# One VectorE operation and two ScalarE passes per weight block, and a written-out order of operations, in a fused attention and gated-MLP kernel

## The chip, the core and the metric

The kernel runs on one core of one Trainium2 chip. The metric is the device time of one execution in microseconds (us); the time given for a kernel is the median of its runs. The engines are TensorE (PE, with its weight loads listed as PEld), VectorE (DVE), ScalarE (ACT), GpSimd (POOL) and SyncE (SP), which issues the transfers. Each engine works through its own instruction list strictly in order, so an instruction that waits holds up everything behind it on that engine.

## The reference

Three stages follow each other. All inputs and the output are 32-bit in the reference; the input arrays arrive as 64-bit floats.

```
k_sum, v_sum = k.blocks(32).max(), v.blocks(32).mean()          # 2 x 8 heads, 768 positions, width 64
scores = [scale * q k^T where |i-j| < 16 else -1e9 , scale * q k_sum^T + log 32]
attn = softmax(scores) @ [v ; v_sum]                             # -> x: 1536 tokens x 512
xn = x / sqrt(mean(x*x) + 1e-6) * rms_g
h  = silu(xn @ w_gate) * (xn @ w_val) ; x = h @ w_out            # 512 -> 1536 -> 512
g  = elu(x @ w_in2) ; out = g @ w_out2                           # 512 -> 2048 -> 512
```

## The kernel before

Tokens are worked in three blocks of 512. Attention goes in pairs of 64-query tiles ("pair" j of batch b): copied keys `ka`, scores `s`, row maxima `nm`, exponentials `e` on ScalarE, a division, a transpose `at` on PE, its copy `ats`, and the product `pv` that is copied into `xT`. The first four pairs make block 0. While blocks 1 and 2 go through attention, block 0 goes through the first MLP (12 chunks: `pg`, `pv_..c` products, gate `th`, down product into `acc`) and the second MLP (16 chunks: `ph`, `ex`, down product into `acc`). Afterwards blocks 1 and 2 go through both MLPs together by a Strassen-Winograd scheme: seven products per unit are added up in the PSUM banks A, B and C (`A_1u` is bank A of the first MLP's up stage, `d` the down stage). Between two products into one bank VectorE or ScalarE reads the bank: B is seeded with A after product 0, `h2` and `h4` are saved from B, and `c11`, then `c10`, are combined from C and `h4`, C and `h2`.

The weights arrive as 64-bit floats, in 68 blocks `st` of 128 x 512. Each is made 32-bit once, for block 0, into `raw`: `convert_a` (ScalarE, line 448) moves the exponent, `convert_b` (VectorE, line 456) shifts the high word by three bits, `convert_d` (VectorE, line 469) adds the rest of the low word. The result is then split into a rounded part (ScalarE, line 317) and a remainder (line 328, on VectorE or POOL), both for PE, and `keep` stores it for the joint stage.

The order on each engine comes from a list scheduler inside the kernel (`Order.issue`): it plays the operations with costs and due times, and a table `SHIFT` moves the due times of operation kinds in time ranges. `keep_warm` puts matmuls on zeros where PE would be idle early.

Of the kernel before, what the change touches and what calls it, by code (L numbers as in the profile page):

```python
# [28 lines left out]
SHARED = (  # L29
    "add_square", "diagonal", "x_lo", "x_hi", "act_a", "act_b", "elu_c", "x_sum", "w_sum", "factor_a", "factor_b",  # L30
    "wide_b", "half_sum", "pair_sum", "pair_b", "gate_b2", "gate_c2", "convert_a", "convert_b", "convert_c",
    "convert_d", "split_a", "split_b", "copy_keys", "normalize")

LIGHT = {"mean_v": 0.7, "mean_own": 0.7, "apply_v2": 0.65}

TILED = {"mean_v": 1, "mean_own": 1, "apply_v2": 2, "scores": 3}  # L40
DRAIN_IN, DRAIN_OUT = 0.12, 0.12


class Order:

    DMA_START, DMA_DONE = 1.3, 1.7
    DONE = {"fetch": 1.9, "keep": 0.7, "keep_sum": 0.7, "load_half": 1.0, "again": 0.9, "store": 0.7, "load_v": 1.2}  # L50
    ISSUE = {"load_vtok": 0.5, "load_v": 0.5}
    TICK, WARM = 3.4133, 1.275

    def __init__(self, look, urgent, busy):
        self.look, self.urgent, self.busy = look, urgent, busy
# [12 lines left out]
    def pe_end(self, now, cost, weight, ticks):

        while cost > 1e-9:  # L70
            k = int(now / self.TICK + 1e-9)
            rate = 1.0 if ticks.get(k - 1, 0) >= self.WARM else 0.5
            part = min(cost, ((k + 1) * self.TICK - now) * rate)
            ticks[k] = ticks.get(k, 0) + part * weight
            cost -= part
            now += part / rate
# [4 lines left out]

    def issue(self):
        ops = self.ops
        n = len(ops)
        before = [set() for _ in range(n)]
        writer, readers, home, maker, users = {}, {}, {}, {}, {}
        queue = {}
        for i, (engine, _, due, _, _, r, w, new) in enumerate(ops):
            for tag, name in new:
                home[name] = tag  # L90
                if tag in self.slots and self.slots[tag][1]:
                    queue.setdefault(tag, []).append((due, i, name))
            for key in r:
                before[i].add(writer[key])
                readers.setdefault(key, []).append(i)
            for key in w:
                if key in writer:
                    before[i].add(writer[key])
                before[i].update(readers.pop(key, ()))
                writer[key] = i  # L100
            before[i].discard(i)
            for name in {key.split("#")[0] for key in (*r, *w)} | {name for _, name in new}:
                if name in home:
                    before[i].add(maker.setdefault(name, i))
                    users.setdefault(name, set()).add(i)
            before[i].discard(i)
        queue = {tag: [name for _, _, name in sorted(x)] for tag, x in queue.items()}
        after = [[] for _ in range(n)]
        left = [len(b) for b in before]
        for i, b in enumerate(before):  # L110
            for j in b:
                after[j].append(i)

        ready_at = [op[2] if op[0] in ("SP", "-") else 0.0 for op in ops]
        free = {tag: bufs for tag, (bufs, _) in self.slots.items()}
        busy, soon, started, port = dict(self.busy), {}, [], 0.0
        dma_free = now = 0.0
        events = [(t, -1, 0) for t in (*ready_at, *busy.values()) if t > 0]
        heapq.heapify(events)
        taken = [None] * n  # L120
        ticks = {}
        tiled = 0

        def offer(i):
            for engine in ops[i][0] if isinstance(ops[i][0], dict) else (ops[i][0],):
                soon.setdefault(engine, []).append(i)

        for i in range(n):
            if not left[i]:
                offer(i)  # L130


        def pick(i):
            need, found = {}, []
            for tags, name in ops[i][7]:
                for tag in tags if isinstance(tags, tuple) else (tags,):
                    n = need.get(tag, 0) + 1
                    if free[tag] >= n and (not self.slots[tag][1] or name in queue[tag][:n]):
                        break
                else:  # L140
                    return None
                need[tag] = n
                found.append((tag, name))
            return found

        def can(i):
            return pick(i) is not None

        def shared(i, engine):
            return engine in ("DVE", "POOL") and ops[i][3].__name__ in SHARED  # L150

        while len(started) < n or events:
            for engine in list(soon):
                if busy.get(engine, 0.0) > now + 1e-9:
                    continue
                todo = sorted((i for i in soon[engine] if taken[i] is None), key=lambda i: (ops[i][2], i))
                best = next((
                    i for i in todo if ready_at[i] <= now + 1e-9 and can(i)
                    and (not shared(i, engine) or port <= now + 1e-9)), None)
                if best is None:  # L160
                    continue
                where, cost, due, _, _, _, _, new = ops[best]
                if isinstance(where, dict):
                    cost = where[engine]
                look = now + self.look * cost
                if engine != "SP" and any(
                        ops[i][2] < due - self.urgent and now < ready_at[i] <= look and can(i) for i in todo):
                    continue
                taken[best] = engine
                for e in where if isinstance(where, dict) else (where,):  # L170
                    soon[e].remove(best)
                for tag, name in pick(best):
                    home[name] = self.tag_of[name] = tag
                    free[tag] -= 1
                    if self.slots[tag][1]:
                        queue[tag].remove(name)
                if engine == "SP":
                    dma_free = max(now + self.DMA_START, dma_free) + cost
                    busy[engine] = now + self.ISSUE.get(ops[best][3].__name__, 0.42)
                    end = dma_free + self.DONE.get(ops[best][3].__name__, self.DMA_DONE)  # L180
                else:
                    if engine == "PE":
                        name = ops[best][3].__name__
                        start = now
                        if TILED.get(name, 0) != tiled:
                            tiled = TILED.get(name, 0)
                            start += DRAIN_IN if tiled else DRAIN_OUT
                        end = self.pe_end(start, cost, LIGHT.get(name, 1.0), ticks)
                    else:
                        end = now + cost  # L190
                    busy[engine] = end
                if shared(best, engine):
                    port = end
                heapq.heappush(events, (end + (0.2 if engine == "PE" else 0.13), best, 1))
                heapq.heappush(events, (busy[engine], -1, 0))
                started.append(best)
                for j in after[best]:
                    left[j] -= 1
                    ready_at[j] = max(ready_at[j], end + self.hop(engine, ops[j][0]))
                    if not left[j]:  # L200
                        offer(j)
                        heapq.heappush(events, (ready_at[j], -1, 0))
# [4 lines left out]
            if ends:  # L207
                for name in {key.split("#")[0] for key in (*ops[i][5], *ops[i][6])} | {x for _, x in ops[i][7]}:
                    if name in users:
                        users[name].discard(i)  # L210
                        if not users[name]:
                            del users[name]
                            free[home[name]] += 1
# [1436 lines left out]
```

## Time and profile before

| | |
|---|---|
| median of 3 runs | 590.2 us (590.08 to 590.88) |
| profiled execution, span of instructions | 589.1 us |
| PE busy | 575.6 us, 98% |
| VectorE busy | 545.4 us, 93% |
| ScalarE busy | 408.6 us, 69% |
| GpSimd busy | 96.2 us, 16% |

An engine is counted busy while an instruction is in it, matmuls with a modelled end, so that a busy PE may still hide short gaps. The span leaves out about 1.1 us that lies around it in the median time.

### The profile page before, as it was taken

What the parts mean: (1) busy time and instruction counts of PE and PEld (TensorE: products, weight loads), DVE (VectorE), ACT (ScalarE), POOL (GpSimd) and SP (SyncE); (2) the same over time, 40 slices, a digit from 0 to 9 for tenths busy, and PEclk for the clock granted to TensorE, in tenths of its full rate; (3) what the DMA queues carried; (4) which work ended last, traced back from release to release, by engine and by line L of the source; (5) the groups of instructions that cost most, each with busy time, mean ns of one, the idle gap of its engine ahead of it and who ended that gap; (6) DMA issues with size and microseconds to landing.
All of it is one profiled execution on the core that took longest, in us unless ns stands there. A gap on an engine that the chain in (4) does not pass through costs nothing.

```text
span 589.1 us, 10067 instructions
## 1 busy us (share of the span) xinstructions
PE 575.6 (98%) x3382; PEld 470.5 (80%) x3382; DVE 545.4 (93%) x1048; ACT 408.6 (69%) x888; POOL 96.2 (16%) x144
## 2 busy tenths in 40 slices
PE   6899999999999999999999999999999999999997
PEld 3688877888788888888888888788888888888886
DVE  4989998889999998999989888999999999999994
ACT  4978749765989889375455446596667599977651
POOL 5755376453311103000000000000000000000000
PEclk9999999999999999999999999999999999999999
DMA  8688899769779799323433453231205525816021
GB/s 312 232 270 305 290 368 327 238 207 298 249 252 303 238 369 333 122 95 121 171 105 118 144 167 120 90 107 55 72 18 203 191 73 170 264 51 214 1 72 53
DMA packets 56052, 108.80 MB, mean 185 GB/s; under 512 B 6784, under 2 KB 19584, under 8 KB 56000
## 3 DMA queue, kind: packets, MB, share of 16 engines
q1 hardware_dynamic: 56000, 108.16, 55.0%
q8 instruction: 26, 0.43, 0.3%
q14 instruction: 26, 0.21, 0.1%
HBM read 79.82 MB, written 28.31 MB: 184 GB/s over the span
## 4 chain that ended last, share of the span: by engine, by line
PE 86%; DVE 6%; DMA 3%; ACT 3%; issue 1%; SPq 0%; POOL 0%; DVEq 0%; POOLq 0%; ACTq 0%
PE acc L966 13%; PE ph L910 8%; PE B_1u L1137 7%; PE B_2u L1137 6%; PE B_2d L1316 6%; PE A_1u L1137 5%; PE C_1u L1137 5%; PE B_1d L1316 4%; PE pg L910 4%; PE A_2u L1137 4%; PE C_2d L1316 4%; PE C_2u L1137 4%; PE A_2d L1316 4%; PE C_1d L1316 3%; PE pv L721 2%; PE A_1d L1316 2%
## 5 line engine op out<-in xcount | busy, mean ns | idle before, releaser
L1137 PE MATMUL B_1u<-xh,w_1u 128*128 128x512 f32 x144 | 48.9, 389 | 0.0
L910 PE MATMUL ph<-xa,ws_i 128*128 128x512 f32 x192 | 45.9, 392 | 0.0
L910 PEld LDWEIGHTS ph<-xa,ws_i 128*128 128x128 f32 x192 | 35.7, 188 | 7.7 <-issue 0.2
L910 PE MATMUL pg<-xs,ws_g 128*128 128x512 f32 (+1 forms) x168 | 37.0, 366 | 0.2 <-DVE th L934 0.2
L1137 PE MATMUL C_1u<-xh,w_1u 128*128 128x512 f32 x96 | 33.4, 390 | 1.1 <-DVE c_1u L1129 1.1
L317 ACT CAST wd<-rd 128x512 fp32r<-128x512 f32 x49 | 29.6, 619 | 5.5 <-PE A_1d L1316 2.8
L1137 PE MATMUL A_1u<-xh,w_1u 128*128 128x512 f32 x96 | 33.1, 389 | 0.0
L328 DVE TENSOR_TENSOR wd<-rd,wd 128x512 fp32r<-128x512 f32 x49 | 33.1, 685 | 0.0
L1137 PE MATMUL B_2u<-xh,w_2u 128*128 128x512 f32 x96 | 32.8, 391 | 0.0
L1316 PE MATMUL B_2d<-td,wd 128*128 128x512 f32 x144 | 32.8, 389 | 0.0
L910 PEld LDWEIGHTS pg<-xs,ws_g 128*128 128x128 f32 x168 | 27.9, 189 | 5.9 <-issue 0.8
L1137 PEld LDWEIGHTS B_1u<-xh,w_1u 128*128 128x128 f32 x144 | 27.0, 188 | 5.6
L1316 PEld LDWEIGHTS B_2d<-td,wd 128*128 128x128 f32 x144 | 27.0, 188 | 5.6
L317 ACT CAST td<-z 128x512 fp32r<-128x512 f32 x28 | 16.7, 620 | 16.9 <-DVE z L1298 16.7
L1137 PE MATMUL B_1u<-xl,w_1u 128*128 128x512 f32 x72 | 28.0, 389 | 0.0
L699 POOL TENSOR_TENSOR e<-e,rs 128x480 f32<-128x480 f32 x20 | 21.1, 1063 | 39.2 <-DVE rs L694 23.8
L684 ACT ACTIVATE e<-e,nm 128x120 f32<-128x120 f32 x64 | 24.4, 384 | 1.0 <-DVE nm L677 0.9
L1316 PE MATMUL B_1d<-td,wd 128*128 128x512 f32 x108 | 24.6, 389 | 0.0
L1316 PEld LDWEIGHTS B_1d<-td,wd 128*128 128x128 f32 x108 | 20.3, 188 | 4.2
L317 ACT COPY h_1u<-B_1u 128x512 f32<-128x512 f32 x22 | 12.9, 588 | 14.8 <-PE B_1u L1137 13.5
L1316 PE MATMUL A_2d<-td,wd 128*128 128x512 f32 x96 | 22.2, 389 | 0.0
L1137 PEld LDWEIGHTS C_1u<-xh,w_1u 128*128 128x128 f32 x96 | 18.0, 188 | 5.3 <-DVE c_1u L1129 1.6
(530 smaller groups left out, 1771.9 us busy)
## 6 DMA issues: line engine op xcount, KB each, us to landing
st_i<-in_moe_w_in SPq DMA_DIRECT2D x16, 512.0 KB, 5.3
st_p<-in_moe_w_out SPq DMA_DIRECT2D x16, 512.0 KB, 5.5
st_v<-in_moe_w_val SPq DMA_DIRECT2D x12, 512.0 KB, 4.8
st_g<-in_moe_w_gate SPq DMA_DIRECT2D x12, 512.0 KB, 6.6
st_o<-in_moe_w_out SPq DMA_DIRECT2D x12, 512.0 KB, 5.0
kept_p<-raw_p SPq DMA_DIRECT2D x16, 256.0 KB, 5.3
kept_i<-raw_i SPq DMA_DIRECT2D x16, 256.0 KB, 5.8
va<-in_v SPq DMA_DIRECT2D x20, 192.0 KB, 6.0
```

Of the source, the lines that this page charges most:

```text
L317: nc.scalar.copy(out=out, in_=in_)
L328: (nc.gpsimd if eng == POOL else nc.vector).tensor_sub(out, a, b)
L684: nc.scalar.activation(out=e[:, pr, :], in_=s[:, pr, :], func=AF.Exp, bias=nm[:, pr:pr + 1], accum_out=ss[:, pr:pr + 1])
L699: nc.gpsimd.tensor_mul(e, e, rs.unsqueeze(2).to_broadcast([P, NP, NK]))
L721: nc.tensor.matmul(pv[64 * h:64 * h + 64, pr, n, :], va[:NK, 2 * pr + h, :], T[f"ats{b}_{j}_{h}"][:, pr, QT * n:QT * n + QT], start=True, ...
L910: nc.tensor.matmul(pt[:, i], wt[:, a, kk * P:(kk + 1) * P], xt[:, c, i], start=(kk == 0 and n == 0), stop=(kk == KM - 1 and n == 2))
L966: nc.tensor.matmul(acc, wt[:, a, cs], ot[e], start=(first and n == 0), stop=(last and n == 2))
L1137: nc.tensor.matmul(pt, wt[:, a, cs], xt[e][:, kk], start=first and kk == n == 0, stop=kk == 1 and n == 2, skip_group_check=not first)
L1316: nc.tensor.matmul(pt[:, h], wt[:, a, cs], xt[:, e, h], start=first and n == 0, stop=last and n == 2 and h.stop == TB, skip_group_check=i ...
```

## The change

`convert_b` and `convert_d` become one VectorE operation, and a second ScalarE pass, `convert_l`, prepares the low word for it: it reads the upper 16 bits of the low word, scales them and writes a whole number of 0 to 7 into the low word's place. The VectorE operation then shifts the high word by three and ORs the two. The scheduler, its costs and `SHIFT` go; `PLAN` lists the operations in order of issue with the chosen engine, `TAGS` the chosen buffers. Costs and due times still stand in the calls but are no longer read. Small edits follow: a new dependency names the selector constants, and the loads of the first queries and weights lose their special cases.

```
-        ops = self.ops
-        n = len(ops)
...
-        for i in started:
-            if i not in later:
-                emit(i)
-        return now
+        picks = iter(TAGS)
+        for code in PLAN:
+            i, choice = divmod(code, 4)
+            engine, _, _, fn, args, _, _, new = self.ops[i]
             for tag, name in new:
...
+                self.tag_of[name] = tag[int(next(picks))] if isinstance(tag, tuple) else tag
+            fn(*((list(engine)[choice],) if isinstance(engine, dict) else ()), *args)
...
+    def convert_l(eng, kind, c):
+        nc.scalar.activation(
+            out=words(kind, c, 0), in_=words(kind, c, 1, U16), func=AF.Copy, scale=0.875 * 2.0 ** -13, bias=0.49)
 
     def convert_b(kind, c):
-        hi = words(kind, c)
-        t = new("raw", f"raw_{kind}{c}", [P, 512], U32)
-        if kind in SIGNED:
-            nc.vector.tensor_scalar(t, hi, 3, None, op0=ALU.logical_shift_left)
...
-    def convert_d(kind, c):
-        rest = T[f"st_{kind}{c}"].bitcast(U16).rearrange("p (n w) -> p n w", w=4)[:, :, 1]
-        low = T[f"raw_{kind}{c}"].bitcast(U16).rearrange("p (n w) -> p n w", w=2)[:, :, 0]
-        nc.vector.scalar_tensor_tensor(low, rest, 2.0 ** -13, low, op0=ALU.mult, op1=ALU.add)
+            new("raw", f"raw_{kind}{c}", [P, 512], U32), words(kind, c), 3, words(kind, c, 0),
+            op0=ALU.logical_shift_left, op1=ALU.bitwise_or)
...
-        add({ACT: 0.57}, 0, need - 8, convert_a, kind, c, r=[st], w=[st])
-        add(DVE, 0.34, need - 7, convert_b, kind, c, r=[st], w=[raw], new=[("raw", raw)])
...
-        add(DVE, 0.63, need - 6, convert_d, kind, c, r=[st, raw], w=[raw])
+        add({ACT: 0.57}, 0, need - 8, convert_a, kind, c, r=[st], w=[st + "#a"])
+        add({ACT: 0.57}, 0, need - 7.5, convert_l, kind, c, r=[st], w=[st + "#l"])
+        add(DVE, 0.63, need - 7, convert_b, kind, c, r=[st + "#a", st + "#l"], w=[raw], new=[("raw", raw)])
...
-SHIFT = {
...
+PLAN = (
+    0, 108, 836, 112, 28, 12, 56, 68, 32, 264, 40, 8, 4, 44, 88, 184, 1648, 64, 60, 76, 72, 48, 52, 196, 189, 194, 80,
...
```

The counts over the whole program, as the built kernels list them: PE has the same 2962 instructions in both. VectorE loses the 68 shifts; 13 of the 29 full-size remainders on POOL move to VectorE (POOL 29 to 16, VectorE's full-size tensor-tensor operations 447 to 460), and so do 3 divisions of exponentials (POOL 20 to 17) and some key copies. ScalarE goes from 791 to 852.

Three places of the order follow. The first is ScalarE in the first attention pairs, from the first key copies to the exponentials of pair 1 (`e_1_0`), before:

```order
L323 ACTIVATE ka_1_266<-ksum_177 128x4x24
L448 ACTIVATE st_v_200<-st_v_200 128x512
L448 ACTIVATE st_g_217<-st_g_217 128x512
L323 ACTIVATE ka_4_309<-kT_0_178 128x4x16
L323 ACTIVATE ka_4_309<-kT_1_190 128x4x80
L323 ACTIVATE ka_4_309<-ksum_177 128x4x24
L684 ACTIVATE e_0_0_278,ss_0_0_321<-s_0_0_262,nm_0_0_301 128x120 x4
L684 ACTIVATE e_0_1_279,ss_0_1_329<-s_0_1_270,nm_0_1_316 128x120 x4
L448 ACTIVATE st_o_221<-st_o_221 128x512
L323 ACTIVATE ka_6_372<-kT_1_190 128x4x96
L323 ACTIVATE ka_6_372<-ksum_177 128x4x24
L684 ACTIVATE e_1_0_341,ss_1_0_389<-s_1_0_296,nm_1_0_365 128x120 x4
```

and in the changed kernel (lines 259 and 262 are `convert_a` and `convert_l`, 467 the exponentials):

```order
L141 ACTIVATE ka_1_238<-ksum_197 128x4x24
L259 ACTIVATE st_v_222<-st_v_222 128x512
L262 ACTIVATE st_v_222<-st_v_222 128x512
L467 ACTIVATE e_0_0_248,ss_0_0_308<-s_0_0_230,nm_0_0_275 128x120 x4
L467 ACTIVATE e_0_1_249,ss_0_1_322<-s_0_1_244,nm_0_1_291 128x120 x4
L262 ACTIVATE st_v_300<-st_v_300 128x512
L259 ACTIVATE st_v_300<-st_v_300 128x512
L467 ACTIVATE e_1_0_337,ss_1_0_360<-s_1_0_268,nm_1_0_358 128x120 x4
```

The key copies `ka_4` and `ka_6` have left ScalarE, and one weight block less is begun, each with two passes.

The second place is ScalarE in the first MLP, around the gates of its chunks 4 and 6 (`th_4`, `th_6`), before:

```order
L448 ACTIVATE st_v_1270<-st_v_1270 128x512
L930 ACTIVATE th_4_1402<-th_4_1402 128x512
L317 CAST ws_g_1423<-raw_g_1399 128x512
L448 ACTIVATE st_o_1360<-st_o_1360 128x512
L317 CAST ws_v_1468<-raw_v_1421 128x512
L317 CAST ws_o_1471<-raw_o_1207 128x512
L317 CAST ws_g_1482<-raw_g_1236 128x512
L317 CAST ws_v_1488<-raw_v_1304 128x512
L448 ACTIVATE st_g_1409<-st_g_1409 128x512
L684 ACTIVATE e_0_0_1429,ss_0_0_1516<-e_0_0_1429,nm_0_0_1480 128x120 x4
L930 ACTIVATE th_6_1514<-th_6_1514 128x512
```

and in the changed kernel, from the gate of chunk 4 to the next attention exponentials (line 713 is the gate):

```order
L262 ACTIVATE st_v_1278<-st_v_1278 128x512
L259 ACTIVATE st_g_1251<-st_g_1251 128x512
L713 ACTIVATE th_4_1291<-th_4_1291 128x512
L259 ACTIVATE st_v_1278<-st_v_1278 128x512
L262 ACTIVATE st_v_1253<-st_v_1253 128x512
L259 ACTIVATE st_v_1253<-st_v_1253 128x512
L467 ACTIVATE e_1_0_1257,ss_1_0_1344<-e_1_0_1257,nm_1_0_1323 128x120 x4
L135 COPY xT_1079<-pv_5_1353 128x4x128
L135 CAST ws_g_1403<-raw_g_1351 128x512
L135 CAST ws_v_1406<-raw_v_1349 128x512
L259 ACTIVATE st_o_1298<-st_o_1298 128x512
L713 ACTIVATE th_5_1398<-th_5_1398 128x512
```

Between gates there are now more conversion passes, and they stand ahead of the casts of later blocks.

The third place is PE at the end of the joint first MLP's up stage, where the last unit's products 5 and 6 go into its bank C (`xh_5`, `xh_6` are the token parts of the products), before:

```order
L1137 MATMUL C_1u_4726<-xh_5_3482,w_1u_4504 128x512
L1137 MATMUL C_1u_4726<-xl_5_3530,w_1u_4504 128x512
L1137 MATMUL C_1u_4726<-xh_5_3482,w_1u_4504 128x512 x2
L1137 MATMUL C_1u_4726<-xl_5_3530,w_1u_4504 128x512
L1137 MATMUL C_1u_4726<-xh_5_3482,w_1u_4504 128x512
L1137 MATMUL C_1u_4726<-xh_6_3560,w_1u_4536 128x512
L1137 MATMUL C_1u_4726<-xl_6_3704,w_1u_4536 128x512
L1137 MATMUL C_1u_4726<-xh_6_3560,w_1u_4536 128x512 x2
L1137 MATMUL C_1u_4726<-xl_6_3704,w_1u_4536 128x512
L1137 MATMUL C_1u_4726<-xh_6_3560,w_1u_4536 128x512
```

and in the changed kernel, from the last matmuls of the last unit's product 5 on:

```order
L920 MATMUL C_1u_4695<-xl_5_3619,w_1u_4467 128x512
L920 MATMUL C_1u_4695<-xh_5_3397,w_1u_4467 128x512
L920 MATMUL C_1u_4622<-xh_6_3615,w_1u_4543 128x512
L920 MATMUL C_1u_4622<-xl_6_3709,w_1u_4543 128x512
L920 MATMUL C_1u_4622<-xh_6_3615,w_1u_4543 128x512 x2
L920 MATMUL C_1u_4622<-xl_6_3709,w_1u_4543 128x512
L920 MATMUL C_1u_4622<-xh_6_3615,w_1u_4543 128x512
L1099 MATMUL A_1d_4661<-td_0_2_4463,wd_01_4682 128x512 x3
L1099 MATMUL A_1d_4719<-td_0_0_4506,wd_00_4631 128x512 x3
L1099 MATMUL A_1d_4719<-td_0_1_4516,wd_00_4631 128x512 x3
```

Product 6 of another unit and ten groups of the down stage's first product now stand between products 5 and 6 of the same bank.

## Rows read from the trace of the kernel before

**Rows 1.** Stretches of the run: busy us and instructions of each engine, PE clock, DMA.
```profile
0.00:44.00 44.00, 35.95 (x498) 26.82 (x499) 33.54 (x83) 30.88 (x113) 25.46 (x67) 0.96 0.81 271
44.00:229.00 185.00, 184.26 (x1315) 150.81 (x1314) 170.55 (x327) 146.18 (x346) 68.16 (x76) 1.00 0.85 290
229.00:260.00 31.00, 31.00 (x142) 25.55 (x141) 29.95 (x62) 17.67 (x33) 2.54 (x2) 1.00 0.38 131
...
400.00:550.00 150.00, 150.00 (x662) 123.64 (x661) 149.94 (x282) 116.06 (x220) 0.00 (x0) 1.00 0.40 129
550.00:589.00 39.00, 35.53 (x163) 29.46 (x161) 30.68 (x52) 14.38 (x24) 0.00 (x0) 0.99 0.13 48
sum 589.00, PE 575.60 PEld 470.46 DVE 545.39 ACT 408.59 POOL 96.17; mean PE 95.93 PEld 78.41 DVE 90.90 ACT 68.10 POOL 16.03
```
**Rows 2.** PE's longest wait that is no first load: us in total, times, longest.
```profile
PE at L709 <- ACT e L684: 2.0, 1, 2.0
```
**Rows 3.** PE at the end of the up stage, and VectorE there, in time.
```profile
378.68 0.39 PE L1137 MATMUL C_1u<-xl,w_1u 128*128 128x512 f32 x1
378.91 0.39 PE L1137 MATMUL C_1u<-xh,w_1u 128*128 128x512 f32 x1
380.44 0.50 PE L1137 MATMUL C_1u<-xh,w_1u 128*128 128x512 f32 x1 [1.14 <-DVE c_1u L1129]
...
379.70 0.68 DVE L1129 TENSOR_TENSOR c_1u<-C_1u,h_1u 128x512 f32<-128x512 f32 x1
```
**Rows 4.** VectorE and then ScalarE in time: conversions and casts that follow each other.
```profile
32.50 0.42 DVE L456 TENSOR_SCALAR raw_v<-st_v 128x512 uint32<-128x512 uint32 x1
32.84 0.42 DVE L456 TENSOR_SCALAR raw_g<-st_g 128x512 uint32<-128x512 uint32 x1
...
33.77 0.74 DVE L469 SCALAR_TENSOR_TENSOR raw_v<-st_v,raw_v 128x512 uint16<-128x512 uint16 x1
34.39 0.73 DVE L469 SCALAR_TENSOR_TENSOR raw_g<-st_g,raw_g 128x512 uint16<-128x512 uint16 x1
...
45.73 0.61 ACT L317 CAST ws_o<-raw_o 128x512 fp32r<-128x512 f32 x1
46.25 0.69 ACT L448 ACTIVATE st_o<-st_o 128x512 f32<-128x512 f32 x1
46.83 0.67 ACT L448 ACTIVATE st_g<-st_g 128x512 f32<-128x512 f32 x1
```
**Rows 5.** GpSimd's remainders: duration in ns (min/median/max), first and last start.
```profile
L328 POOL TENSOR_TENSOR ws_g<-raw_g,ws_g x12: 1278/1298/1698, 39.4 to 139.5; 128x512 fp32r<-128x512 f32 x12
```
**Rows 6.** ScalarE's `convert_a` alone (line 448): busy us and count, PE clock, DMA.
```profile
44.00:229.00 185.00, 39.51 (x60) 1.00 0.85 290
229.00:260.00 31.00, 1.35 (x2) 1.00 0.38 131
```
**Rows 7.** ScalarE before its first exponentials, and PE in the opening, in time.
```profile
11.79 0.60 ACT L323 ACTIVATE ka<-kT 128x64 f32<-128x64 f32 x2
...
12.47 0.34 ACT L684 ACTIVATE e<-s,nm 128x120 f32<-128x120 f32 x1
...
9.66 1.05 PE L668 MATMUL s<-ka,q 64*64 64x120 f32 x32
...
27.66 1.25 PE L709 MATMUL at<-ident,e 128*120 128x128 f32 x8 [1.96 <-ACT e L684]
```
**Rows 8.** Two stretches of the opening, columns as in the first group.
```profile
28.00:30.00 2.00, 2.00 (x29) 1.67 (x29) 1.70 (x7) 1.57 (x7) 0.51 (x2) 0.60 0.00 0
30.00:32.00 2.00, 2.00 (x26) 1.55 (x24) 0.80 (x2) 0.97 (x2) 1.54 (x2) 0.55 0.32 103
```
**Rows 9.** What ScalarE waited for between 44 and 229 us: total, times, longest.
```profile
ACT ws_v L317 <- DVE raw_v L469: 7.0, 5, 3.0
ACT xT L317 <- PE pv L721: 4.8, 2, 4.5
ACT th L930 <- DVE th L927: 4.6, 4, 2.2
```

More of the change, by code (lines that the diff above doesn't have):

```diff
@@ L25, with __init__ @@
 NEG = -1000000000.0
[L29 to L41, printed above, removed]
-class Order:
[L49 to L55, printed above, removed]
+class Order:
+    def __init__(self):
         self.ops = []
@@ L63, in add @@
     def add(self, engine, cost, due, fn, *args, r=(), w=(), new=()):
-        due += SHIFT.get((fn.__name__, sum(due >= x for x in EDGES)), 0)
         self.ops.append((engine, cost, due, fn, args, tuple(r), tuple(w), tuple(new)))
[L68 to L76, printed above, removed]
-        return now
@@ L79, in hop @@
-    def hop(self, a, b):
-        return (0.0 if a == b else 0.2) if a == "PE" else 0.13
-    def issue(self):
-        ops = self.ops
-        n = len(ops)
[L85 to L88, printed above, removed]
-            for tag, name in new:
[L90 to L202, printed above, removed]
-            if not events:
-                stuck = [(e, [(ops[i][2], ops[i][3].__name__, ops[i][4][:3]) for i in t[:3]]) for e, t in soon.items()]
-                raise RuntimeError(f"no group can start: {stuck} {free}")
-            now, i, ends = heapq.heappop(events)
[L207 to L213, printed above, removed]
-        def find(name, *some):
-            return next(i for i in started if ops[i][3].__name__ == name and set(some) <= set(map(str, ops[i][4])))
-        held = {}
-        for late, first in HOLD:
-            held.setdefault(find(*first), []).append(find(*late))
-        later = {j for x in held.values() for j in x}
-        def emit(i):
-            ops[i][3](*((taken[i],) if isinstance(ops[i][0], dict) else ()), *ops[i][4])
-            for j in held.get(i, ()):
-                emit(j)
-        for i in started:
-            if i not in later:
-                emit(i)
-        return now
@@ L254, in fused_kernel @@
     log_b = math.log(BLOCK)
-    o = Order(LOOK, URGENT, {"POOL": 2.1, "DVE": 3.1, "ACT": 2.0, "SP": 0.8})
+    o = Order()
     add = o.add
@@ L381, in fused_kernel @@
     for var in (1, 0, 2):
-        add(POOL, 1.5, 5.0 + var, make_mask, var, r=[] if var == 1 else ["mask1"], w=[f"mask{var}"])
+        add(POOL, {1: 1.5, 0: 0.46, 2: 2.86}[var], 5.0 + var, make_mask, var, r=[] if var == 1 else ["mask1"], w=[f"mask{var}"] + ["sel"] * (var == 2))
     for var in range(2):
@@ L473, in add_weights @@
         add("SP", 1.6, need - (14 if need > T0 + 20 else LEAD), fetch, kind, c, w=[st], new=[("st", st)])
-        add({ACT: 0.57}, 0, need - 8, convert_a, kind, c, r=[st], w=[st])
-        add(DVE, 0.34, need - 7, convert_b, kind, c, r=[st], w=[raw], new=[("raw", raw)])
-        if kind not in SIGNED:
-            add(DVE, 0.6, need - 6.5, convert_c, kind, c, r=[st, raw], w=[raw])
-        add(DVE, 0.63, need - 6, convert_d, kind, c, r=[st, raw], w=[raw])
+        add({ACT: 0.57}, 0, need - 8, convert_a, kind, c, r=[st], w=[st + "#a"])
+        add({ACT: 0.57}, 0, need - 7.5, convert_l, kind, c, r=[st], w=[st + "#l"])
+        add(DVE, 0.63, need - 7, convert_b, kind, c, r=[st + "#a", st + "#l"], w=[raw], new=[("raw", raw)])
         add("SP", 0.67, need + KEEP, keep, kind, c, r=[raw], w=[f"kept_{kind}{c}"])
@@ L539, in add_k @@
             kt = f"kT{b}_{j}"
-            add("SP", 1.4, due - 4 + 1.5 * j, load_first, b, j, w=[kt], new=[("x", kt)])
+            add("SP", 1.4, due - 4 + 1.5 * j, load_k, b, j, w=[kt], new=[("x", kt)])
             for r in range(2):
@@ L747, in add_pair @@
             near = [f"kT{b}_{x}" for x in range(lo // (2 * P), (hi - 1) // (2 * P) + 1)]
-            add({POOL: 0.78, DVE: 0.45, ACT: 0.65} if early else [{POOL: 0.78}, {POOL: 0.78, ACT: 0.65}][KEYS if i >= FLEX else 0], 0, due, copy_keys, b, t,
+            add({POOL: 0.86, DVE: 0.45, ACT: 0.65} if early else [{POOL: 0.86}, {POOL: 0.86, ACT: 0.65}][KEYS if i >= FLEX else 0], 0, due, copy_keys, b, t,
                 r=near + far, w=[f"ka{b}_{t}"], new=[("ka", f"ka{b}_{t}")])
@@ L767, in add_pair @@
                 w=[f"e{n}", f"ss{n}"], new=[("ss", f"ss{n}")])
-            add(DVE, 0.08, at + 4, guard, b, f"{j}_{h}", w=[f"ss{n}"])
+            add(DVE, 0.13, at + 4, guard, b, f"{j}_{h}", w=[f"ss{n}"])
             add(DVE, 0.1, at + 4, invert, b, f"{j}_{h}", r=[f"ss{n}"], w=[f"rs{n}"], new=[("rs", f"rs{n}")])
@@ L1095, in half_sum @@
     def half_sum(sa, sb, blocks, dst):
-        a11, a12, a21, a22 = (part(x) for x in blocks)
+        a11, a12, a21, a22 = blocks
         name, i = (sa, int(dst[1]) - 1) if dst in ("s1", "s2") else (sb, int(dst[1]) - 3)
@@ L1429, in fused_kernel @@
     add("-", 0.0, 0, take, "act", "rk0", [P, TB], w=["rk0"], new=[("act", "rk0")])
-    for i, at in enumerate(WARM_AT):
-        add("-", 0.0, at, wait, w=[f"w{i}"])
-        add(PE, 0.44, at, keep_warm, i, r=[f"w{i}"], new=[(BANKS, f"warm{i}")])
     for i in range(VA):
@@ L1435, in fused_kernel @@
     add_k(0, K0, 0.7)
+    for i, at in enumerate(WARM_AT):
+        add(PE, 0.44, at, keep_warm, i, r=[f"kT0_{AFTER_K[i]}"] if i in AFTER_K else [], new=[(BANKS, f"warm{i}")])
     add_vsum(0, VS0, VS0 + MEAN, BANKS)
```

176 lines of the change are left out of this document (15 added, 161 removed), and 150 rows, old and new, of the table PLAN.

## The prediction

> **What bounds the kernel.** I read the stretches of the run first, then PE's waits, then single places in time. In the stretches the reader is to see that PE is the bound: it is busy 575.6 of 589 us, and what is left lies at the two ends: 8.05 us of PE idle before 44, 0.74 between 44 and 229, none from 400 to 550 although VectorE is busy 149.94 of 150 us there, and 3.47 in the last 39 [rows 1]. PE's list holds the same 2962 matmuls in both kernels, so the time can fall only by PE's idle, by gaps too short to show as idle, and by time at a low clock. A matmul of 128 x 512 shows 0.39 us and the next one starts 0.23 us after it, so a gap of up to 0.16 us is hidden in "busy" [rows 3]. PE's longest wait that is no first load is 2.0 us on exponentials in the opening [rows 2]. The longest in the joint stages is 1.14 us of idle for VectorE's combine of bank C, from start to start 380.44 - 378.91 - 0.23 = 1.30 us [rows 3].
>
> **The conversion.** Two VectorE shifts that follow each other start 0.34 us apart, two `convert_d` 0.62 us apart [rows 4]. The new VectorE operation is not in this trace. It is a pass over 512 elements like both: the bounds are 0.34 (as cheap as the shift) and 0.74 (a whole `convert_d`, nothing overlapped). I take 0.62, since it reads two sources, as `convert_d` does. So the shift alone is saved: 68 x 0.34 = 23.1 us of VectorE; the bounds make it 15 to 42. The Trainium skill, "VectorE: DVE Perf Modes", section "The perf-mode tier table", says that a 32-bit operation on one source runs at twice the rate of one on two, so the change would remove the cheap member of the pair. The rows agree, 0.34 beside 0.62; by that rule the saving would be an estimated 68 x 0.31 = 21 us in place of 23.
>
> The second ScalarE pass is not in this trace either. The nearest row is `convert_a`, a pass over the same strided block: 0.58 us from start to start. Bounds: 0.52, a cast's spacing, and 0.69, a `convert_a` with nothing overlapped [rows 4]. I take 0.58, as reading and writing every other word is what the two share: 68 x 0.58 = 39.4 us more ScalarE (35 to 47).
>
> **The order.** The 13 remainders that move from POOL (1.30 us each, [rows 5]) take about 0.68 us on VectorE, as its combine does [rows 3], or 0.62 in a row, so 8.1 us; for the 3 divisions and some small key copies I put 4 us, by an estimate from their sizes at the same time per element. VectorE's net is -23.1 + 8.1 + 4 = -11 us. None of this is PE time by itself: VectorE full to the brim from 400 to 550 cost PE nothing [rows 1]. The further ScalarE time is hidden too, as long as ScalarE has idle to put it in.
>
> That cover, stage by stage. Between 44 and 229 ScalarE is busy 146.2 of 185 us [rows 1], and 60 of the 68 `convert_a` run there [rows 6]. As many second passes are 60 x 0.58 = 34.8 us, which gives 181.0 of 185, or 98%, if everything stayed in its place. With the next 31 us, where it is busy 17.7 us and two more run, it is 199.8 of 216, or 92%. So the room is there only if the order spreads work towards 260 and keeps ScalarE's waits small. The order does put passes between gates and ahead of later casts, as the second place of the order shows; what queues behind a waiting ScalarE instruction there are gates, exponentials and casts that PE needs soon. I charge PE +0.4 us for the middle (bounds -1, if POOL's slower remainders no longer delay a product, to the rival's +6 below).
>
> Opening. Before its first exponentials at 12.47 ScalarE does the key copies of `ka_4` from 11.79 [rows 7]; these have left it, which frees 0.68 us on the chain of scores, maximum and exponentials. The further load up to pair 3's exponentials I take as even: a block less is begun, each with two passes. The wait of 1.96 us for pair 2's exponentials ended at 27.66 [rows 7], and after it PE's clock was granted at 0.60 and 0.55 for 4 us [rows 8], on the mean between its levels of 2.4 and 1.2 GHz; work that would fill 4 x 0.575 = 2.3 us at full rate took 4, a loss of 1.7. In the new order eight of the matmuls on zeros, which stood ahead of the first scores, stand just between `pv_0` and pair 2's transposes, so PE is kept at work in that very gap. They cost nothing if the exponentials are still late, and up to 8 x 0.23 = 1.8 us if not. Against the gains: the first scores (1.05 us for 32, [rows 7]) now come after fewer such matmuls and might run at the lower level, +1.0. I take -0.7 - 1.7 + 1.0 = -1.4 us; bounds -3.7 (both the 1.96 of wait and the 1.7 of clock go) and +2 (the zeros are not covered).
>
> End of the up stage. Product 6 went into bank C directly behind product 5, with a VectorE read of C between them: the 1.30 us, which no free VectorE could have saved. Now product 6 of another unit and ten groups of three matmuls stand there, over 35 x 0.23 = 8 us, against the 0.68 us that the combine takes. So -1.3. At the tightest product change that is left, any bank has six matmuls in between, 6 x 0.23 = 1.4 us, twice the combine. I add -0.4 for the shorter gaps that this removes (bounds 0 to -0.6).
>
> Sum: -1.4 + 0.4 - 1.3 - 0.4 = -2.7 on the profiled 589.1, so a span of 586.4; with the 1.1 us that lie outside it, 587.5 against the median of 590.2. I predict 587.5. Its own range, with these terms near their taken values, is 586 to 589.
>
> **Rivals.** *All of it is gained.* Opening -3.7, middle -1, late -1.9 together are -6.6: 583.6. For it: PE's longest wait and its low clock lie together in the opening. Against it: the chain of exponentials stays, in the same order.
>
> *ScalarE becomes the bound between 44 and 260.* The 181.0 of 185 us leave 4.0 us, and ScalarE's three largest waits in that stretch alone are 16.4 us [rows 9]. They are waits for VectorE and PE, partly filled now by passes that need only a load. If half of them, 8.2 us, cannot be filled and nothing moves behind 229, PE waits 8.2 - 4.0 = 4.2 us there in place of the 0.4: 587.5 + 4.2 - 0.4 = 591.3; if none can be filled, 16.4 - 4.0 = 12.4, 599.5. It decides from 4.0 + 0.4 + 2.7 = 7.1 us of unfilled waits on: from there the kernel is not faster. Moving 5 us of casts or passes behind 229 takes it away again, and that stretch has 13.3 us of ScalarE idle [rows 1]. The Trainium skill, "ScalarE: Activation LUTs", section "Rules for kernel authors", speaks for this rival: it gives scaling and adding to VectorE, not ScalarE.
>
> *The two cancel.* The opening is fixed by loads and by the chain of exponentials, the gap at 26 us is only moved, and ScalarE costs 1 to 2 us: 589 to 591. For it: the wait that ends at 27.66 hangs on a chain that is as long as before.
>
> **Chances.** Forecast 0.44, all gained 0.16, cancel 0.17, ScalarE the bound 0.23. A measurement of this kernel tells some 0.2% (1.2 us) from no change. Forecast and all gained lie below 589.0, nearly always: faster 0.59. Cancel, with the mild end of the ScalarE case, gives same 0.18; the rest, slower 0.23. The range leaves out the lowest tenth and the cases of ScalarE far over: 583.5 to 594.
>
> **What would show it.** Right: ScalarE near 92 to 95% busy between 44 and 260, and in all about 39 us more than its 408.6; VectorE's busy time down by 10 to 25; no wait on bank C near 379; PE's clock at 1.00 through 28 to 32; PE idle before 44 down by a microsecond or two. Wrong: PE waiting for casts `ws` or exponentials between 44 and 229, or many small waits that show in the spacing of matmuls; the second pass at more than 0.7 us; the eight matmuls on zeros run while exponentials already lie ready.

## The result, and the profile after

The changed kernel takes 595.4 us in the median of 6 runs (593.5 to 599.1) against 591.1 us for the kernel before beside it: ratio 1.0079, 95% interval 1.0055 to 1.0103. It is 0.8% slower; 587.5 was predicted, at most 594. The profiled execution took 594.5 us with a span of 592.8, 3.7 us above the span before. Single executions of one kernel lie about 1% apart (the kernel before: 589.6 to 595.0 on one chip), so fractions of a per cent are read from the ratios.

The stretches of the run answer to [rows 1], with the same columns:

```profile
0.00:44.00 44.00, 37.09 (x532) 28.74 (x532) 36.09 (x96) 34.76 (x116) 19.20 (x55) 0.96 0.89 307
44.00:229.00 185.00, 180.68 (x1267) 147.12 (x1267) 153.91 (x286) 166.74 (x389) 54.60 (x66) 0.99 0.81 278
229.00:260.00 31.00, 31.00 (x138) 25.22 (x137) 29.06 (x55) 25.59 (x49) 0.00 (x0) 1.00 0.44 146
260.00:400.00 140.00, 140.00 (x619) 115.77 (x618) 130.40 (x246) 75.96 (x146) 0.00 (x0) 1.00 0.38 117
400.00:550.00 150.00, 149.10 (x658) 122.89 (x657) 147.81 (x275) 116.99 (x224) 0.00 (x0) 1.00 0.46 139
550.00:592.80 42.80, 39.28 (x179) 32.24 (x177) 33.56 (x57) 16.90 (x32) 0.00 (x0) 1.00 0.14 51
sum 592.80, PE 577.15 PEld 471.99 DVE 530.83 ACT 436.94 POOL 73.80; mean PE 96.19 PEld 78.66 DVE 88.47 ACT 72.82 POOL 12.30
```

The loss is in one stretch. PE's idle went from 8.05 to 6.91 us before 44, from 0.74 to 4.32 between 44 and 229, from 1.14 (bank C) to nothing between 260 and 400, and from nothing to 0.90 between 400 and 550. ScalarE is busy 166.7 of 185 us between 44 and 229, 90%, so it is not full there. What PE waited for names the place (the longest wait that is a first load left out):

```profile
PE at L492 <- POOL e L482: 3.8, 1, 3.8
...
PE A_2u L920 <- DVE c_2u L912: 0.9, 1, 0.9
```

One wait of 3.8 us, for GpSimd. The chain of waits from 80 to 110 us shows where it comes from. The chain is followed back from the end, at each step to what released an instruction or to what stood ahead of it on its engine, and is printed in order of time (start, us, what).

```profile
104.51 0.56 DVE nm L460
...
105.09 0.04 DVE va L137
...
106.17 1.05 POOL va L364
...
107.30 1.31 POOL e L482
...
108.65 0.65 PE at L492 x4
```

PE's transposes (`at`) wait for a division of exponentials on GpSimd (line 482). The division did not wait for its own data. GpSimd and VectorE in time, over the same stretch:

```profile
100.56 0.18 DVE L477 RECIPROCAL rs<-ss 128x4 f32<-128x4 f32 x1
...
102.97 0.17 DVE L477 RECIPROCAL rs<-ss 128x4 f32<-128x4 f32 x1
...
105.09 0.92 DVE L137 COPY va<-vm 24x128 f32<-24x128 f32 x4
...
87.09 1.44 POOL L482 TENSOR_TENSOR e<-e,rs 128x480 f32<-128x480 f32 x1
106.17 1.04 POOL L364 TENSOR_SCALAR va<-va 24x512 f32<-24x512 f32 x1 [17.64 <-DVE va L137]
107.30 1.30 POOL L482 TENSOR_TENSOR e<-e,rs 128x480 f32<-128x480 f32 x1
```

GpSimd stood idle for 17.64 us in front of line 364. That is the repeat of the mean rows of batch 1 (`va0` into another `va`), which waits for a VectorE copy (line 137). The copy is at the end of a full VectorE list and starts at 105.09. The division stands behind the repeat in GpSimd's list, and its reciprocals, the first of the two in the rows, had been ready since 100.74. So it started 6.6 us later than it could. The order of the two kernels on GpSimd at this place, which the prediction never looked at: before, from the repeats to the divisions of batch 1,

```
L581 TENSOR_SCALAR va_171<-va_170 24x512
L581 TENSOR_SCALAR va_172<-va_170 24x512
L581 TENSOR_SCALAR va_173<-va_170 24x512
...
L699 TENSOR_TENSOR e_0_0_1429<-e_0_0_1429,rs_0_0_1555 128x480
...
L699 TENSOR_TENSOR e_0_1_1430<-e_0_1_1430,rs_0_1_1588 128x480
```

and in the changed kernel, where repeats and divisions alternate (both lists are cut at the dots):

```
L482 TENSOR_TENSOR e_1_1_1258<-e_1_1_1258,rs_1_1_1520 128x480
L364 TENSOR_SCALAR va_195<-va_281 24x512
L482 TENSOR_TENSOR e_0_1_1414<-e_0_1_1414,rs_0_1_1685 128x480
L364 TENSOR_SCALAR va_187<-va_281 24x512
```

So before, too, the divisions stood behind repeats that wait for a VectorE copy. There the copy came early: the repeats ran at 81.58, 11 us ahead of the first of these divisions.

```profile
81.58 3.04 POOL L581 TENSOR_SCALAR va<-va 24x512 f32<-24x512 f32 x3 [1.25 <-DVE va L319]
...
93.02 0.98 POOL L699 TENSOR_TENSOR e<-e,rs 128x480 f32<-128x480 f32 x1
```

The wait cost more than its 3.8 us, as the stretches behind it show (columns as above, PE's granted clock third from the end):

```profile
110.00:112.00 2.00, 2.00 (x6) 1.53 (x6) 0.00 (x0) 2.00 (x4) 1.22 (x4) 0.50 0.99 339
112.00:114.00 2.00, 2.00 (x10) 1.61 (x9) 0.32 (x1) 1.25 (x3) 0.00 (x0) 0.67 0.43 165
```

After the idle PE ran at 0.50 and 0.67, the lower of its two levels for much of 4 us: 2 x 0.50 + 2 x 0.33 = 1.7 us lost. Change of PE's idle over the stretches (-1.14 + 3.58 - 1.14 + 0.90 + 0.05 = 2.25) and this 1.7 give 3.9, against 3.7 of span. The price in clock is no matter of this one execution: over the whole span the mean granted clock is 0.989 to 0.997 in all ten executions of the changed kernel (six here, four in its second run below), and 0.996 to 1.000 in the ten of the first experiment, which takes the wait away (medians 0.9925 and 0.999).

### The profile page after: what moved, and what is told of

It reads as the page before. It is cut to its first block, busy times and chain, and to the rows that moved or that the text cites. A ratio compares the mean times of both kernels' runs of the same rounds, so it can differ in the third digit from the quotient of the medians.

```text
span 592.8 us, 9930 instructions
## 1 busy us (share of the span) xinstructions
PE 577.2 (97%) x3382; PEld 472.0 (80%) x3382; DVE 530.8 (90%) x1010; ACT 436.9 (74%) x949; POOL 73.8 (12%) x121
## 4 chain that ended last, share of the span: by engine, by line
PE 84%; ACT 7%; DVE 5%; DMA 2%; issue 1%; POOL 0%; SPq 0%; DVEq 0%; ACTq 0%; POOLq 0%
PE acc L749 12%; PE B_1u L920 8%; PE ph L693 8%; PE B_2d L1099 6%; PE A_1u L920 6%; PE C_1u L920 6%; PE B_2u L920 4%; PE B_1d L1099 4%; PE C_2d L1099 4%; PE A_2d L1099 4%; PE pg L693 4%; PE C_2u L920 3%; PE A_2u L920 3%; PE C_1d L1099 3%; PE A_1d L1099 3%; PE pv L504 1%
## 5 line engine op out<-in xcount | busy, mean ns | idle before, releaser
L693 PE MATMUL ph<-xa,ws_i 128*128 128x512 f32 x192 | 47.1, 395 | 0.0
L693 PE MATMUL pg<-xs,ws_g 128*128 128x512 f32 (+1 forms) x168 | 38.8, 379 | 0.5 <-DVE th L717 0.5
L1099 PE MATMUL B_2d<-td,wd 128*128 128x512 f32 x144 | 35.7, 391 | 0.0
L482 POOL TENSOR_TENSOR e<-e,rs 128x480 f32<-128x480 f32 x17 | 19.3, 1138 | 57.1 <-DVE rs L477 49.2
L1099 PE MATMUL B_1d<-td,wd 128*128 128x512 f32 x108 | 25.9, 390 | 0.0
L1099 PE MATMUL A_2d<-td,wd 128*128 128x512 f32 x96 | 24.4, 389 | 0.0
L1099 PE MATMUL C_2d<-td,wd 128*128 128x512 f32 (+1 forms) x102 | 24.3, 377 | 0.0
```

The costliest lines, as they stand in the source:

```text
L482: nc.gpsimd.tensor_mul(e, e, rs.unsqueeze(2).to_broadcast([P, NP, NK]))
L693: nc.tensor.matmul(pt[:, i], wt[:, a, kk * P:(kk + 1) * P], xt[:, c, i], start=(kk == 0 and n == 0), stop=(kk == KM - 1 and n == 2))
L1099: nc.tensor.matmul(pt[:, h], wt[:, a, cs], xt[:, e, h], start=first and n == 0, stop=last and n == 2 and h.stop == TB, skip_group_check=i ...
```

## The experiments

Two theories. **Q**: the loss is this one division behind the repeat in GpSimd's queue. **S**: the second ScalarE passes make ScalarE the bound (the prediction's rival), and the wait at 105 is where it surfaces. Ratios are to the kernel before on the same chip, with the 95% interval.

**The division ahead of the repeat** (one entry of the list moved by one place):

```diff
-    ..., 856, 864, 992, ...
+    ..., 856, 992, 864, ...
```

> The changed kernel with one entry of its list moved: GpSimd's division of the exponentials e1_0_1 stands ahead of the repeat of the mean rows into va2, which waits for a VectorE copy. Theory Q (the loss is this one place in GpSimd's queue): PE's wait of 3.8 us near 105 and the low clock behind it go, 4 to 5.5 us less, 590 to 591.5. Theory S (ScalarE is the bound between 44 and 260, and the wait only surfaces here): PE waits elsewhere within the next 30 us, at most 1.5 us are gained, 594 or more.

590.46 us, ratio 0.9981 (0.9958 to 1.0003); span 587.5. By the ratios that is 0.98%, 5.8 us, less than the changed kernel (5.3 us in the spans of the profiled executions), about as Q has it. PE from 103.5 on, and GpSimd, in that run:

```profile
103.77 0.39 PE L749 MATMUL acc<-act_2h,ws_o 128*128 128x512 f32 x1
104.00 0.60 PE L492 MATMUL at<-ident,e 128*120 128x128 f32 x4
104.36 2.99 PE L693 MATMUL pg<-xs,ws_g 128*128 128x512 f32 x12
...
100.17 1.29 POOL L482 TENSOR_TENSOR e<-e,rs 128x480 f32<-128x480 f32 x1 [12.35 <-DVE rs L477]
106.26 2.07 POOL L364 TENSOR_SCALAR va<-va 24x512 f32<-24x512 f32 x2 [4.79 <-DVE va L137]
```

The division starts at 100.17, right behind its reciprocals, and PE goes from the down product into the transposes without a gap. The repeat still waits until 106.26, and PE does not feel it. Whether an earlier VectorE copy would do as well was not run; in the changed kernel the copy's source (`vm`, a ScalarE copy of 0.24 us at 101.25) was there 3.6 us before the copy started.

**No second pass.** The low bits of the weights are left out, so ScalarE is relieved; the order is the changed kernel's.

```diff
     def convert_l(eng, kind, c):
-        nc.scalar.activation(
-            out=words(kind, c, 0), in_=words(kind, c, 1, U16), func=AF.Copy, scale=0.875 * 2.0 ** -13, bias=0.49)
+        pass
...
-            new("raw", f"raw_{kind}{c}", [P, 512], U32), words(kind, c), 3, words(kind, c, 0),
+            new("raw", f"raw_{kind}{c}", [P, 512], U32), words(kind, c), 3, idle_w.bitcast(U32)[:, :1].to_broadcast([P, 512]),
```

> The changed kernel without the second ScalarE pass (the low bits of the weights are left out: the VectorE operation ORs zeros in their place), in the changed kernel's order. ScalarE has about 39 us less. Theory Q: the division still stands behind the repeat, which stands behind the same VectorE list; the wait near 105 stays within 1 us, 593.5 to 595. Theory S: the wait goes with ScalarE's load, 589 to 590.5.

593.76 us, ratio 1.0034 (1.0017 to 1.0050). The wait is there, just as long:

```profile
PE at L491 <- POOL e L481: 3.8, 1, 3.8
```

The time lies in Q's range, and this speaks against S as the cause of the wait: with ScalarE at 138 of 185 us between 44 and 229, in place of 167, PE waits the same 3.8 us. The passes are not free here, though: the ratio is 0.45%, 2.7 us, under the changed kernel's 1.0079, and the two intervals do not overlap. The profiled executions (spans 592.2 and 592.8) do not show where the 2.7 us lie.

**Both at once** (the first entry moved, and no second pass):

> The kernel with the division first, and without the second ScalarE pass (the low bits of the weights are left out, zeros are ORed in their place). It gives what 39 us of ScalarE still cost once the division is out of the way. Theory Q: at most 1.5 us, since ScalarE fits into its idle time: 589 to 590.5. Theory S: the passes are the cost, and without them the kernel falls to 586 or less.

588.89 us, ratio 0.9968 (0.9956 to 0.9979): just under Q's 589, and far from the 586 of S. Against 0.9981 with the passes the 68 passes cost about 0.13%, 0.8 us; the intervals overlap, so it may be nothing or 2.5 us. ScalarE's busy time is 401.7 us in all against 436.9, which prices the passes at 35.2 us, 0.52 each.

**The new conversion in the old order** (the kernel before, with both passes where `convert_a` stood and the one VectorE operation where `convert_d` stood):

```diff
             nc.scalar.activation(out=hi, in_=hi, func=AF.Prelu, scale=2.0 ** -112, alpha=-2.0 ** 32)
+            nc.scalar.activation(out=x, in_=y, func=AF.Copy, scale=0.875 * 2.0 ** -13, bias=0.49)
...
-            nc.vector.tensor_scalar(t, hi, 3, None, op0=ALU.logical_shift_left)
+            pass
...
-        nc.vector.scalar_tensor_tensor(low, rest, 2.0 ** -13, low, op0=ALU.mult, op1=ALU.add)
+        nc.vector.scalar_tensor_tensor(
+            T[f"raw_{kind}{c}"], words(kind, c), 3, low, op0=ALU.logical_shift_left, op1=ALU.bitwise_or)
```

> The kernel before in its own order with the new conversion alone: two ScalarE passes where convert_a stood, the one VectorE operation where convert_d stood, nothing where the shift stood. Theory Q: the conversion by itself costs little, since VectorE gets 23 us back, 590 to 593. Theory S: an order that leaves no room for the second passes is worse than the changed one, 596 to 605, with ScalarE over 95% busy from 44 to 229 and many small waits of PE.

599.72 us, ratio 1.0132 (1.0102 to 1.0161): Q's number is wrong, and S is right in the time and in the many small waits, not in the load (ScalarE at 90%, where over 95% was expected). VectorE got its time back (521.5 us in all against 545.4), and the kernel lost 1.3%, 7.8 us. No wait is long. What PE waited for between 44 and 260:

```profile
PE at L712 <- POOL e L702: 1.6, 3, 0.8
PE ph L913 <- ACT ws_i L317: 1.4, 1, 1.4
PE pv L724 <- ACT ats L317: 1.3, 1, 1.3
```

The stretch from 44 to 229, columns as before:

```profile
44.00:229.00 185.00, 178.35 (x1281) 143.29 (x1280) 143.71 (x260) 166.81 (x391) 64.19 (x74) 1.00 0.81 274
```

PE's idle in this stretch is 6.65 us, where the kernel before had 0.74. ScalarE is at 90% as in the changed kernel, but its passes stand ahead of things that PE needs, and PE waits a little for casts, copies and divisions. So the passes are not free in every order. The run moves the passes and the VectorE operation together and does not tell their shares apart.

**The old conversion in the new order** (shift and old VectorE operation together, no second pass):

```diff
     def convert_l(eng, kind, c):
-        nc.scalar.activation(
-            out=words(kind, c, 0), in_=words(kind, c, 1, U16), func=AF.Copy, scale=0.875 * 2.0 ** -13, bias=0.49)
+        pass
...
-        nc.vector.scalar_tensor_tensor(
-            new("raw", f"raw_{kind}{c}", [P, 512], U32), words(kind, c), 3, words(kind, c, 0),
-            op0=ALU.logical_shift_left, op1=ALU.bitwise_or)
+        t = new("raw", f"raw_{kind}{c}", [P, 512], U32)
+        nc.vector.tensor_scalar(t, words(kind, c), 3, None, op0=ALU.logical_shift_left)
+        rest = words(kind, c, 1, U16)
+        low = t.bitcast(U16).rearrange("p (n w) -> p n w", w=2)[:, :, 0]
+        nc.vector.scalar_tensor_tensor(low, rest, 2.0 ** -13, low, op0=ALU.mult, op1=ALU.add)
```

> The changed kernel in its order with the old conversion: no second pass, the shift and the old VectorE operation together where the new one stands, so 23 us more VectorE and 39 us less ScalarE than in the changed kernel. Theory Q: the division stays behind the repeat, and the VectorE copy that the repeat waits for comes no earlier, 594 to 598. Theory S: 589 to 591.

609.88 us, ratio 1.0310 (1.0279 to 1.0341), outside both numbers. The wait for the division is 4.8 us, so Q's part holds, and waits for VectorE come on top:

```profile
PE at L493 <- POOL e L483: 4.8, 1, 4.8
PE pg L694 <- DVE th L718: 1.7, 2, 1.3
...
PE pg L694 <- DVE ws_g L146: 1.4, 1, 1.4
```

VectorE is busy 568.4 us in all. So the new order needs the cheaper conversion (3.1% slower without it, and still with the late division), and the new conversion needs the new order (1.3% slower without it).

**The products of the last bank C together again** (with the division first; the combine and product 6 moved up to product 5):

```diff
-    ..., 6232, ..., 6520, ..., 6260, ..., 6264, ...
+    ..., 6232, 6260, 6264, ..., 6520, ...
```

> The kernel with the division first, and at the end of the up stage product 6 of the last bank C straight behind product 5, with the combine between them, as in the kernel before. If the change's order there is worth what the prediction says, PE waits 1.0 to 1.2 us on that combine and the kernel is 1.3 to 1.7 us slower, span 588.8 to 589.2. Rival: the waits move, less than 0.4 us.

592.73 us, ratio 1.0020 (1.0006 to 1.0034), by the ratios 0.39% or 2.3 us above the same kernel without this edit. PE waits, in the place of the edit and behind it:

```profile
PE B_1d L1099 <- ACT B_1d L135: 1.0, 1, 1.0
...
PE C_1u L920 <- DVE c_1u L912: 0.8, 1, 0.8
```

The combine's wait returns, and the down products that had stood between now run into a later wait for a bank seed. Together they are 1.8 us, where PE had no idle between 260 and 400 without the edit. So this part of the change gains about what was said for it (1.3 and 0.4 us). The profiled execution, 595.1 us, is the slowest of this run; it also holds a wait of 1.8 us, in place of 0.8, for the combine near 480 that is treated below.

**The eight matmuls on zeros left out** (with the division first):

```diff
-AFTER_K, WARM_LONG = {1: 0, 2: 2}, {1: 8}
+AFTER_K, WARM_LONG = {1: 0, 2: 2}, {1: 0}
```

> The kernel with the division first, and without the eight matmuls on zeros between pv0_0 and pair 2's transposes. If they keep PE's clock up, as the prediction has it, PE waits 1 to 2 us on exponentials there, the granted clock falls in the 4 us behind it, and the kernel is 1 to 2 us slower, 591.5 to 592.5. Rival: the exponentials were ready by then and the eight only delayed PE: 0.5 to 1.7 us faster, no fall of the clock.

590.05 us, ratio 0.9973 (0.9954 to 0.9991): no difference from 0.9981 that can be told, so neither forecast of the time came true. Pair 2's transposes start at 25.99, right behind the product, in place of 27.16: the exponentials of the first four had lain ready, and the eight matmuls stood in front of them. PE is idle 8.93 us before 44 without them and 6.94 with them, at the same time of the kernel. The granted clock did not fall behind the gap without them (it fell later, to 0.51 and 0.64 from 36 to 40):

```profile
26.00:28.00 2.00, 1.35 (x31) 1.14 (x32) 2.00 (x3) 1.94 (x10) 1.92 (x3) 1.00 0.53 162
28.00:30.00 2.00, 1.99 (x51) 1.52 (x46) 1.90 (x6) 2.00 (x11) 1.51 (x5) 1.00 0.93 256
30.00:32.00 2.00, 1.68 (x36) 1.43 (x36) 1.97 (x7) 2.00 (x5) 0.75 (x2) 1.00 0.84 272
```

**Five matmuls on zeros ahead of the first scores** (with the division first):

```diff
-AFTER_K, WARM_LONG = {1: 0, 2: 2}, {1: 8}
+AFTER_K, WARM_LONG = {1: 0, 2: 2}, {1: 8, 2: 5}
```

> The kernel with the division first, with five matmuls on zeros behind the second key load in place of two, so that PE is at work for 1.3 us more ahead of the first scores. If the first scores are slow (1.64 us for 32 in place of 1.05) because PE had done little ahead of them, they take 1.05 and everything up to pair 3 comes 0.5 us earlier. Rival: the five delay the first scores by 1 us, and the opening is 0.5 to 1 us longer.

590.20 us, ratio 0.9979 (0.9966 to 0.9992). The first 32 scores take 1.05 us and start at 9.67, and the next ones start at 12.60 in place of 13.20 (with the division first alone). That this comes from the five matmuls is not shown: the run without the eight, which has only two there, shows 1.05 at 9.73 and 12.66 too, and in the other profiled executions with the division first and the passes the 32 take 1.12 to 1.88 us. At the end nothing of it is left.

**The wait of 0.9 us near 480.** Three kernels, each with the division first. The combine moved up in VectorE's list, ahead of the half-sum and the two operations behind it (three operations, nine entries of the whole list):

```diff
-    ..., 9564, ..., 8704, ...
+    ..., 8704, 9564, ...
```

> The kernel with the division first (590.46, span 587.5), and in VectorE's list the combine c10_2u3 moved ahead of the second half-sum of sa_2d5, five places up, so that it no longer stands behind a half-sum that waits for a reloaded weight. Theory: PE's wait of 0.8 us on that combine (1.1 us from start to start) goes, span 586.4, and the time stands 0.3 to 0.5% under the kernel before. Rival: the half-sums and remainders that are pushed back by 0.6 us make a later product wait, no gain.

589.70 us, ratio 0.9977 (0.9963 to 0.9991), span 587.4: the wait on the combine is gone, and PE waits for a remainder `w_2u` close by (0.3 us and gaps too short to show). Of the span of 586.4 that was expected nothing came, as the rival has it. Two reloads ahead of three stores in SP's list:

```diff
-    ..., 9556, 9544, 9552, 9548, 9516, 9236, ...
+    ..., 9556, 9552, 9236, 9544, 9548, 9516, ...
```

> The kernel with the division first, and in SP's list the reloads of ra_2d5 and rb_2u7 ahead of the three stores of half-sums (the stores wait for VectorE, and the reloads stood behind them). Theory: the half-sum that waits 0.2 to 1.0 us for rb_2u7 near 473 waits no more, the combine behind it comes in time, PE's wait of 0.8 us on it goes, and the spread of the executions shrinks: 1.1 us less, span 586.4. Rival: the stores, put back, hold buffers that the next reloads need, no gain.

591.31 us, ratio 1.0018 (0.9994 to 1.0042). The rival came true, VectorE now waits for the buffer that a store still reads:

```profile
473.42 0.43 DVE L885 TENSOR_TENSOR sb_2u<-ra_2u,rb_2u 128x256 f32<-128x256 f32 x1 [0.75 <-DMA kept_sa_2d<-sa_2d]
```

Both edits together:

> The division first, the two reloads first, and the combine c10_2u3 five places up in VectorE's list. Expected as the reloads alone or 0.2 us better: span 586.2 to 586.5, 0.3 to 0.5% under the kernel before. Rival: none of the two is worth anything, as the division first alone (0.998).

591.34 us, ratio 1.0010 (1.0001 to 1.0019): as the reloads alone, and no gain over the division first, so the expected 0.3 to 0.5% did not come. How to get rid of this wait stays open.

**The changed kernel once more**, beside the last three:

> The changed kernel as it is, beside the next three on one chip. Both theories: 0.6 to 1.0% slower than the kernel before, with the wait of about 4 us near 105 in its profile again.

595.81 us, ratio 1.0088 (1.0069 to 1.0107), with the wait of 3.8 us for the division at the same place and the clock at 0.50 and 0.68 from 110 to 114. In the opening its clock differs from the first profile's 0.70 and 0.50:

```profile
34.00:36.00 2.00, 2.00 (x35) 1.98 (x36) 1.43 (x4) 2.00 (x5) 0.00 (x0) 1.00 0.86 272
36.00:38.00 2.00, 1.77 (x50) 1.34 (x45) 1.98 (x6) 2.00 (x5) 0.76 (x1) 1.00 0.96 381
```

## Why the prediction was wrong

The step that failed is "I charge PE +0.4 us for the middle". It measured 3.6 us of idle and 1.7 us of clock, 5.3 in all, by the mechanism that the run with the division first takes away: PE's idle there is 0.45 us in it, and 5.3 us of span are gained. The prediction asked what queues behind a waiting instruction on ScalarE alone; the wait was on GpSimd, whose list had become shorter (13 of its 29 full-size remainders had left it, and its busy share fell from 16% to 12%). A short list can still stop PE, here because one of its entries waited for a VectorE copy that came late.

The other steps, by the rows:

- The conversion. Two of the new VectorE operations start 0.59 us apart, two ScalarE passes 0.57:

```profile
100.65 0.68 DVE L266 SCALAR_TENSOR_TENSOR raw_o<-st_o 128x512 uint32<-128x512 uint32 x1
101.24 0.69 DVE L266 SCALAR_TENSOR_TENSOR raw_g<-st_g 128x512 uint32<-128x512 uint32 x1
...
100.10 0.67 ACT L259 ACTIVATE st_o<-st_o 128x512 f32<-128x512 f32 x1
100.67 0.67 ACT L262 ACTIVATE st_o<-st_o 128x512 uint32<-128x512 uint16 x1
```

  0.62 and 0.58 were taken: right. VectorE's busy time fell by 14.6 us (11 predicted). ScalarE's rose by 28 against the 39 predicted: the passes take 35, and 7 us of other work left ScalarE.
- The rival "ScalarE becomes the bound" had the sign, not the main mechanism: without its passes the changed kernel still waits 3.8 us and is still 0.34% slower than the kernel before. ScalarE is 89% busy between 44 and 260, under the 92 to 95% that were to speak for the forecast. The passes have a share: without them the changed kernel gains 2.7 us by the ratios, and in the old order the conversion alone makes the kernel 1.3% slower. The Trainium skill, "ScalarE: Activation LUTs", section "Rules for kernel authors", which gives scaling to VectorE, speaks against the pass. The runs bear it out in the old order; with the new order and the division first the passes cost 0.8 us, which may be nothing.
- Opening, -1.4 predicted: PE's idle fell by 1.1 us, and pair 2's transposes start at 27.11 in place of 27.66. The wait of 1.96 us is gone and the clock stays at 1.00 from 28 to 32, as predicted, but not for the reason given: it stays there without the eight matmuls too, and the eight ran while exponentials lay ready, which the prediction had named as a sign of being wrong. In this execution the low clock is only moved, to 34 to 38, and costs 0.6 + 1.0 = 1.6 us there, as much as before:

```profile
34.00:36.00 2.00, 2.00 (x37) 1.89 (x36) 1.41 (x5) 2.00 (x5) 0.00 (x0) 0.70 0.96 337
36.00:38.00 2.00, 2.00 (x35) 1.67 (x33) 2.00 (x6) 2.00 (x6) 0.76 (x1) 0.50 1.03 417
```

  The term of 1.7 us for the clock was read from one execution, and it is not tied to the order. The second profile of the changed kernel has no low clock here, and the kernel with the old order has none behind its wait of 1.97 us for the same exponentials:

```profile
28.00:30.00 2.00, 1.10 (x10) 0.96 (x10) 2.00 (x5) 2.00 (x13) 1.36 (x3) 1.00 0.43 141
30.00:32.00 2.00, 1.26 (x33) 1.12 (x34) 1.63 (x6) 1.94 (x6) 1.15 (x2) 1.00 0.15 28
```

  Of 75 more executions of the kernel before, 28 have a mean granted clock of 0.996 or 0.997 over the span (the stretches of the profiled one give about the same), and 47 have 0.999 or 1.000. The slower first scores were foreseen (+1.0); they took 1.67 in place of 1.05 us, and 1.05 to 1.88 in the executions with the division first.
- Bank C, -1.3: the wait is gone, and putting the products back costs 2.3 us with the down products' new wait behind it. Right in kind and, within the noise, in size.
- The last -0.4: not there; a new wait of 0.9 us came in its place near 480, on a combine that stands behind work for a reloaded weight. No run shows the gain from shorter gaps by itself.

Without the one division the sum would have been nearer: 590.46 is 0.19% under the kernel before, where -0.5% was predicted, with an interval that just reaches no change. No version here that does the whole work beats the kernel before by more than 0.3%.

## What to carry to other kernels

When an order is written out for every engine, follow each engine that PE waits for, also the one with the shortest list: an entry that waits for a copy from elsewhere is a gate for all that stands behind it, and moving one entry by one place was worth 5 to 6 us here. A pass that is moved to an idle engine costs what the order makes of it: 0.8 to 2.7 us in the new order, while in the old one the whole conversion lost 7.8 us. A wait on TensorE can have a second price behind it in the granted clock, here 1.7 us after 3.8. Behind a wait of 2.0 us it was there in one profile and not in another, so a term for the clock should not be read from one execution.

## What was not expected of the hardware

In the first profile of the changed kernel PE's granted clock fell to 0.70 and 0.50 between 34 and 38 us although PE shows as busy all of the 4 us; before the fall it had done many small matmuls (53 records in the 2 us from 30, then 16 of four columns until 34.4). In the second profile of the same kernel it did not fall there. The other way round, in the first microseconds the clock column shows 1.00 while the matmuls run slowly. PE in time, in the changed kernel:

```profile
8.04 1.05 PE L1210 MATMUL warm<-idle_w 128*128 128x512 bf16 x2
...
9.58 1.67 PE L451 MATMUL s<-ka,q 64*64 64x120 f32 x32
...
25.82 1.46 PE L1210 MATMUL warm<-idle_w 128*128 128x512 bf16 x6
```

The clock column of the stretch:

```profile
8.00:11.00 3.00, 3.00 (x40) 2.06 (x38) 1.25 (x6) 1.51 (x3) 0.42 (x2) 1.00 1.04 388
```

Two matmuls on zeros take 1.05 us at 8.04, and six take 1.46 us at 25.82. The 32 scores take 1.67 us at 9.58 and 1.05 at 13.15. Their durations, not the column, show the slow start.
